# Attention with dense layers on one core: queries loaded by whole tiles, values by pairs of heads, stores of converted weights issued by GpSimd

## The chip, the core and the metric

The kernel runs on one core of a Trainium2 chip. The core has five engines that matter here, each with its own queue of instructions in program order: TensorE (PE in the profile; its weight loads, which run beside the matmuls, are PEld), VectorE (DVE), ScalarE (ACT), GpSimd (POOL) and SyncE (SP), which computes nothing and only issues transfers. An instruction waits on semaphores for what it reads and for the buffers that it writes. The metric is device microseconds (us) from start to end of one execution, the median of the runs of a kernel. The profile is of one execution, with the span in which its engines work and the clock that was granted to TensorE.

## The reference

Attention for two batches of eight heads, 576 positions and 64 numbers a head. Of each row of scores only the 32 largest go into the softmax. The result, 1152 rows of 512 features, passes through two dense layers (512 to 2048 to 512 features), the first with a softplus between its two products, the second with a leaky rectifier that has a slope for each of the 2048 features.

```
scores = scale * (q @ k.transpose(0, 1, 3, 2))        # q, k, v: 2 x 8 x 576 x 64, float32
kth    = np.partition(scores, -32, axis=-1)[..., -32:-31]
scores = np.where(scores >= kth, scores, -1e9)
attn   = np.exp(scores - scores.max(-1)) ; attn = attn / (attn.sum(-1) + 1e-9)
x = (attn @ v) as 1152 x 512
h = x @ w_in                                          # 512 x 2048, float64
x = (np.maximum(h, 0) + np.log1p(np.exp(-np.abs(h)))) @ w_out    # 2048 x 512, float64
h = x @ w_in2 ; out = (np.maximum(h, 0) + alpha * np.minimum(h, 0)) @ w_out2
```

The four weight matrices come as float64. Their bits are handed to the core unchanged, as two 32-bit words for each number, and the core makes float32 of them.

## The kernel before

**Tiles and stages.** The 1152 rows are nine tiles of 128. `CHUNKS` puts them into three chunks: tiles 3 and 4, tiles 5 to 7, and tiles 8, 0, 1, 2. A chunk first goes through attention, then through the first dense layer, then through the second, while the rows of the next chunk go through attention beside them. One "row" of the program is one head of one tile, so a chunk of two tiles has sixteen rows. Chunk 0 multiplies in float32 (`NATIVE`); the two others split each operand into a high and a low part and use three products.

**A row of attention.** TensorE makes the scores of two heads from a query tile `q` and a key tile `ks` (L430, `pss`), ScalarE copies them out (L435, `s`). VectorE finds the 32 largest with four MAX8 (L439, `m`) and three MATCH_REPLACE8 between them that strike out those already found (L442, `r`). ScalarE or VectorE builds a mask from the 32nd (L476, L478), GpSimd subtracts it in two halves (L481, `e`), ScalarE takes the exponential (L483). TensorE transposes `e` (L497 and L503, `pp` and `pq`), ScalarE copies that to `pt` (L500, L504), and TensorE multiplies it by the values `v` for two heads at a time (L527, `pav`). After the eighth head the sums of the rows are inverted by VectorE, spread by TensorE (L574, `pr`), copied by ScalarE (L578, `xn`) and multiplied by VectorE into the tile's features: `xh`, L581 in chunk 0. The first matmul of the first dense layer (`ph`, L623) needs the `xh` of both tiles of chunk 0.

**The weights.** `convert` takes one of 32 units of 128 x 1024 numbers. SyncE loads its raw bits, 1024 KB, into `cr` (L317); VectorE shifts and masks the high words into `cx` (L320) and keeps two low bits of them (L325); ScalarE turns the low words into 16 bits (L327); GpSimd adds the two in four pieces of 256 columns (L331). SyncE then stores the result, 512 KB, to a scratch tensor `ws` in the chip's memory (L334), from which later chunks load it into `w` (L359). Of the units 24 are converted ahead of the layer that uses them first (`EARLY`), the others as they are needed, and used from `cx` too.

**Buffers.** Raw bits `cr` have two (`RAWB`), `cx` three (`CXB`), `w` four (`RING`), scores `s` eight, queries `q` six tiles of 64 KB (`QB`), keys `ks` five (`KB`), values `v` ten tiles of 160 KB (`VB`), `e` two. A load into a buffer waits on its queue until the last reader of what stands there is done, and everything behind it on that queue waits with it.

**What sets the order.** The functions below don't run their instructions; they hand them to a `Planner` with an engine, a length, a due time, what they read and write, and for transfers the bytes. `order` then goes through all engines by a simple model of time and lets each take, of what could start, the one with the earliest due time. The result is the order of each engine's queue, kept as it is. Due times come from the numbers at the top (`T0`, `PACE`, `ROWS_DUE`, `AHEAD`, the leads), so these set which conversion stands ahead of which row.

Of the kernel before, what the change touches and what calls it, by code (L numbers as in the profile page):

```python
# [19 lines left out]
P = 128  # L20
# [14 lines left out]
CHUNKS = [[3, 4], [5, 6, 7], [8, 0, 1, 2]]  # L35
RING = 4
# [5 lines left out]
QB = 6  # L42
KB = 5
VB = 10
# [3 lines left out]
SPARE = [-17033.9, 2009.0, 903.3]  # L48
MASK_SPARE = [24031.0, 784.7, -18754.5]
# [5 lines left out]
T0 = 229.4  # L55
VALUES = 1.35
SCORES = 0.69
PACE = [1433.1, 1301.1, 6152.8, 6484.8, 326.6, 8896.4]
ROWS_DUE = [(-1910.7, -760.0), (978.8, 846.5), (2800.8, 12532.4)]
EARLY_DUE = [-2160.8, -143.0, 2538.2]  # L60
LOAD_LEAD = 3880.4
FETCH_LEAD = [364.0, 1458.3, -965.3]
# [205 lines left out]
def topk_attention_moe_kernel(ctx: ExitStack, tc: tile.TileContext, q, k, v, w1, w2, w3, w4, alpha, out):  # L268
# [4 lines left out]
    plan = Planner()  # L273
    op = plan.op
# [19 lines left out]
    begins = [T0 + sum(PACE[:i]) for i in range(2 * len(CHUNKS))]  # L294
# [16 lines left out]
    def convert(unit, due):  # L311
# [22 lines left out]
        op("SP", 0.45, due, lambda: nc.sync.dma_start(z, f().bitcast(F32)), reads=[f], writes=[f"ws{nm}"],  # L334
# [171 lines left out]
    def values(i):  # L506
# [23 lines left out]
        op("PE", VALUES * len(parts), due, products, reads=[*pts] + [vt for vts, _, _ in parts for vt in vts], writes=[av],  # L530
# [67 lines left out]
    class Layer:  # L598
# [3 lines left out]
        def __init__(self, layer, ci):  # L602
            self.layer, self.ci, self.tiles = layer, ci, CHUNKS[ci]
# [4 lines left out]
            self.turned = layer == 0 and ci == len(CHUNKS) - 1 and not self.native  # L608
# [46 lines left out]
        def down(self, j):  # L655
# [40 lines left out]
            if self.layer == 0:  # L696
# [123 lines left out]
```

## Time and profile before

| What | Value |
| --- | --- |
| median of three runs | 687.59 us (685.85 to 687.65) |
| the profiled execution's own time | 689.61 us |
| its span | 687.7 us |
| TensorE's mean granted clock | 0.938 of full speed |
| TensorE busy | 620.6 us, 90% of the span |
| VectorE busy | 544.3 us, 79% |
| ScalarE busy | 485.3 us, 71% |
| GpSimd busy | 359.6 us, 52% |
| moved by the DMA engines | 109.59 MB, mean 159 GB/s |

The span begins with the first work that the profile shows and ends with the last; the time of the execution is 1.9 us longer. The shares are means over a program whose stages differ: no engine need be the bound everywhere. In a timeline each row begins with its start in us, its length, its engine and its line; the brackets at its end hold the idle time ahead of it and what ended that. "x4" counts instructions taken together, and under a tile's or a line's name the durations are in ns.

### The profile page before, as it was taken

What the parts mean: (1) busy time and instruction counts of PE and PEld (TensorE: products, weight loads), DVE (VectorE), ACT (ScalarE), POOL (GpSimd) and SP (SyncE); (2) the same over time, 40 slices, a digit from 0 to 9 for tenths busy, and PEclk for the clock granted to TensorE, in tenths of its full rate; (3) what the DMA queues carried; (4) which work ended last, traced back from release to release, by engine and by line L of the source; (5) the groups of instructions that cost most, each with busy time, mean ns of one, the idle gap of its engine ahead of it and who ended that gap; (6) DMA issues with size and microseconds to landing.
All of it is one profiled execution on the core that took longest, in us unless ns stands there. A gap on an engine that the chain in (4) does not pass through costs nothing.

```text
span 687.7 us, 10318 instructions
## 1 busy us (share of the span) xinstructions
PE 620.6 (90%) x3432; PEld 463.7 (67%) x3432; DVE 544.3 (79%) x1024; ACT 485.3 (71%) x975; POOL 359.6 (52%) x393
## 2 busy tenths in 40 slices
PE   5746545699999999999999999999999999999997
PEld 3424434466666566568877778878888888788885
DVE  4999999999999899999999999989545544554442
ACT  3877678698869778878888888788675655533431
POOL 0575666565575469766987677868411112121120
PEclk9686655699999999999999999999999999999999
DMA  8877667778978883842332312122142232313121
GB/s 286 283 250 232 196 215 216 239 238 269 305 266 309 248 271 108 269 148 84 123 108 92 106 50 93 62 93 92 62 168 95 91 112 72 121 63 123 61 92 61
DMA packets 34324, 109.59 MB, mean 159 GB/s; under 512 B 3936, under 2 KB 12128, under 8 KB 30176
## 3 DMA queue, kind: packets, MB, share of 16 engines
q1 hardware_dynamic: 34272, 108.94, 47.7%
q8 instruction: 27, 0.44, 0.3%
q14 instruction: 25, 0.20, 0.1%
HBM read 89.79 MB, written 19.14 MB: 158 GB/s over the span
## 4 chain that ended last, share of the span: by engine, by line
PE 67%; DVE 12%; DMA 7%; POOL 5%; issue 4%; ACT 4%; SPq 1%; POOLq 0%; DVEq 0%; ACTq 0%
PE ph L594 8%; PE pa L594 8%; PE pa L596 8%; PE pa L595 8%; PE ph L596 8%; PE ph L595 8%; DMA cr<-in_w_dram 6%; PE pa L671 5%; DVE m L439 4%; PE pss L430 4%; DVE r L442 4%; PE ph L623 4%; PE pp L497 3%; POOL cx L331 3%; DVE cr L325 2%
## 5 line engine op out<-in xcount | busy, mean ns | idle before, releaser
L439 DVE MAX8 m<-r 128x8 f32<-128x576 f32 x216 | 156.2, 747 | 0.4
L481 POOL TENSOR_TENSOR e<-s,e 128x288 f32<-128x288 f32 x144 | 122.6, 862 | 40.1 <-ACT e L476 28.4
L331 POOL TENSOR_TENSOR cx<-cx,cr 128x256 int32<-128x256 int32 x128 | 98.8, 792 | 83.3 <-ACT cr L327 61.5
L343 POOL TENSOR_TENSOR w<-w 128x512 fp32r<-128x512 f32 x68 | 92.3, 1367 | 79.3 <-ACT w L349 75.6
L442 DVE MATCH_REPLACE8 r<-m,r 128x576 f32<-128x576 f32 x144 | 106.4, 741 | 0.0
L343 POOL TENSOR_TENSOR gl<-g,gh 128x384 fp32r<-128x384 f32 (+1 forms) x40 | 46.4, 1160 | 100.6 <-ACT gh L651 100.4
L430 PE MATMUL pss<-ks,q 64*128 64x288 f32 x320 | 75.7, 531 | 19.7 <-ACT s L435 11.9
L327 ACT ACTIVATE cr<-cr 128x1024 int16<-128x1024 uint32 x32 | 80.0, 2500 | 17.4 <-DVE cr L325 17.2
L497 PE MATMUL pp<-ident,e 128*128 128x128 f32 x288 | 48.4, 301 | 34.6 <-ACT e L483 21.9
L349 ACT CAST w<-w 128x1024 fp32r<-128x1024 f32 x64 | 66.9, 1045 | 11.1 <-DMA w<-ws 10.9
L497 PEld LDWEIGHTS pp<-ident,e 128*128 128x128 f32 x288 | 37.1, 153 | 52.7 <-ACT e L483 26.6
L430 PEld LDWEIGHTS pss<-ks,q 64*128 64x128 f32 x320 | 35.5, 219 | 48.8 <-ACT s L435 19.3
L594 PE MATMUL pa<-w,gh 128*128 128x512 f32 x160 | 66.9, 418 | 0.0
L435 ACT COPY s<-pss 128x288 f32<-128x288 f32 x144 | 52.0, 406 | 19.6 <-PE pss L430 15.6
L595 PE MATMUL pa<-w,gl 128*128 128x512 f32 x160 | 63.3, 396 | 0.0
L596 PE MATMUL pa<-w,gh 128*128 128x512 f32 x160 | 63.2, 395 | 0.0
L483 ACT ACTIVATE e<-e,nb 128x576 f32<-128x576 f32 x72 | 55.6, 772 | 9.0 <-POOL e L481 9.0
L344 DVE TENSOR_TENSOR w<-w 128x512 fp32r<-128x512 f32 x60 | 45.1, 787 | 18.6 <-ACT w L349 18.6
L638 DVE SCALAR_TENSOR_TENSOR g<-ph,g 128x256 f32<-128x256 f32 (+2 forms) x48 | 26.6, 554 | 42.1 <-ACT g L637 40.9
L439 DVE MAX8 m<-s 128x8 f32<-128x576 f32 x72 | 53.0, 746 | 8.2 <-ACT s L435 8.0
L442 DVE MATCH_REPLACE8 r<-m,s 128x576 f32<-128x576 f32 x72 | 53.4, 741 | 0.0
L644 DVE SCALAR_TENSOR_TENSOR g<-g,rest,ph 128x256 f32<-128x256 f32 (+2 forms) x48 | 29.2, 608 | 30.4 <-ACT g L642 28.3
(127 smaller groups left out, 1389.2 us busy)
## 6 DMA issues: line engine op xcount, KB each, us to landing
w<-ws SPq DMA_DIRECT2D x88, 512.0 KB, 3.3
cr<-in_w_dram SPq DMA_DIRECT2D x32, 1024.0 KB, 7.4
ws<-cx SPq DMA_DIRECT2D x32, 512.0 KB, 7.6
v<-in_v_dram SPq DMA_DIRECT2D x24, 160.0 KB, 4.3
ks<-in_k_dram SPq DMA_DIRECT2D x12, 288.0 KB, 4.3
q<-in_q_dram SPq DMA_DIRECT2D x40, 64.0 KB, 4.1
out_dram<-o SPq DMA_DIRECT2D x9, 256.0 KB, 2.0
al<-in_alpha_dram SPq DMA_DIRECT2D x1, 8.0 KB, 2.8
```

What stands on the lines that cost most here:

```text
L327: op("ACT", ACT_LOW, due, lambda: nc.scalar.activation(raw().bitcast(I16)[:, :, 2], low(), AF.Copy, scale=2.0 ** -29), reads=[f], writes=[ ...
L331: op("POOL", on_pool(cs.stop - cs.start), due, lambda cs=cs: nc.gpsimd.tensor_add(f().bitcast(I32)[:, cs], f().bitcast(I32)[:, cs], high() ...
L343: lambda cs=cs: nc.gpsimd.tensor_sub(lo()[:, cs], x()[:, cs], hi()[:, cs].bitcast(F32)),
L349: op("ACT", on_act(WIDE), due, lambda: nc.scalar.copy(w()[:, 0, :], x()), reads=reads, writes=[w])
L430: nc.tensor.matmul(pss[n](), qr()[n * D:(n + 1) * D, :], ks()[n * D:(n + 1) * D, cs], start=j == 0, stop=j == len(qk) - 1)
L439: op("DVE", on_dve(n), due, lambda: nc.vector.max(out=out(), in_=x()), reads=reads, writes=writes)
L442: op("DVE", on_dve(n) + 0.067, due, lambda: nc.vector.match_replace(out=out(), in_to_replace=found(), in_values=x(), imm_value=LOWEST), re ...
L481: op("POOL", on_pool(HS), due - AHEAD["mask"][ci], lambda cs=cs: nc.gpsimd.tensor_sub(e()[:, cs], s()[:, cs], e()[:, cs]), reads=[s], writ ...
L497: nc.tensor.transpose(pp()[:, c * P:(c + 1) * P], e()[:, c0 + c * P:c0 + (c + 1) * P], ident)
L594: nc.tensor.matmul(acc, ah, b_l, start=first, stop=False)
L595: nc.tensor.matmul(acc, a_l, bh, start=False, stop=False)
L596: nc.tensor.matmul(acc, ah, bh, start=False, stop=last)
```

## The change

Six things are different.

- **Queries.** One load brings the queries of all four pairs of heads of a tile, 256 KB, where one load brought one pair, 64 KB. Tile 4, which lies in both batches, has two. There are ten such loads instead of forty, and two buffers of 256 KB instead of six of 64.
- **Values.** One load brings both heads of a pair, 320 KB, where one load brought one head, 160 KB: twelve loads instead of 24, five buffers of 320 KB instead of ten of 160. On the host `vp` is laid out so that such a block is contiguous.
- **Stores.** The 32 stores `ws<-cx` are issued by GpSimd (`STORER`). In the planner's model such an issue takes 1.0 us there, on SyncE 0.45. All loads stay on SyncE (`LOADER`).
- **The planner's numbers.** Nearly all of them are different, so each engine's queue has another order.
- **`TOGETHER`.** The second dense layer could now take several chunks at once. With `[[0], [1], [2]]` it takes each by itself, as before.
- **Line numbers** move: L317 is now L325, L334 is L342, L581 is L594, L623 is L637.

```diff
+TOGETHER = [[0], [1], [2]]
+LOADER = 'SP'
+STORER = 'POOL'
+ISSUE = {"SP": 0.45, "ACT": 0.45, "POOL": 1.0}
...
-QB = 6
+QB = 2
...
-VB = 10
+VB = 5
...
-T0 = 229.4
+T0 = 118.9
...
+    loader, storer = ({"SP": nc.sync, "ACT": nc.scalar, "POOL": nc.gpsimd}[x] for x in (LOADER, STORER))
...
-        op("SP", 0.45, due, lambda: nc.sync.dma_start(z, f().bitcast(F32)), reads=[f], writes=[f"ws{nm}"],
+        op(STORER, ISSUE[STORER], due, lambda: storer.dma_start(z, f().bitcast(F32)), reads=[f], writes=[f"ws{nm}"],
...
-        op("SP", 0.45, due + AHEAD["scores"][ci] - LOAD_LEAD, lambda: nc.sync.dma_start(ks(), k[b, pair]), writes=[ks],
-           move=P * S * 4)
-
-    def prepare_v(b, h, ci, due):
-        if (b, h) in vst:
+        op(LOADER, ISSUE[LOADER], due + AHEAD["scores"][ci] - LOAD_LEAD, lambda: loader.dma_start(ks(), k[b, pair]),
+           writes=[ks], move=P * S * 4)
+
+    def prepare_v(b, pair, ci, due):
+        if (b, pair) in vst:
             return
         if len(vst) == VB:
             del vst[next(iter(vst))]
-        vst[b, h] = vt = buf("v", VB, [P, 5, D], F32, f"v{b}{h}")
-        op("SP", 0.45, due + AHEAD["values"][ci] - LOAD_LEAD / 2, lambda: nc.sync.dma_start(vt(), v[b, h]), writes=[vt], move=P * 5 * D * 4)
+        vst[b, pair] = vt = buf("v", VB, [P, 2, 5, D], F32, f"v{b}{pair}")
+        op(LOADER, ISSUE[LOADER], due + AHEAD["values"][ci] - LOAD_LEAD / 2, lambda: loader.dma_start(vt(), v[b, pair]),
+           writes=[vt], move=P * 10 * D * 4)
+
+    def prepare_q(t, n, ci, due):
+        if (t, n) in qst:
+            return
+        qst[t, n] = qr = buf("q", QB, [P, H // 2, P], F32, f"q{t}_{n}")
+        op(LOADER, ISSUE[LOADER], due + AHEAD["scores"][ci] - LOAD_LEAD, lambda: loader.dma_start(
+            qr(), q[:, NT if n else t]), writes=[qr], move=P * H // 2 * P * 4)
...
             prepare_k(b, pair, ci, due)
-            qr = buf("q", QB, [P, P], F32, f"q{t}{pair}{n}")
-            op("SP", 0.45, due + AHEAD["scores"][ci] - LOAD_LEAD, lambda n=n, qr=qr: nc.sync.dma_start(
-                qr(), q[:, NT if n else t, pair]), writes=[qr], move=P * P * 4)
-            qk.append((qr, kst[b, pair]))
+            prepare_q(t, n, ci, due)
+            qk.append((qst[t, n], kst[b, pair]))
...
-                        nc.tensor.matmul(pss[n](), qr()[n * D:(n + 1) * D, :], ks()[n * D:(n + 1) * D, cs],
+                        nc.tensor.matmul(pss[n](), qr()[n * D:(n + 1) * D, pair, :], ks()[n * D:(n + 1) * D, cs],
...
-            prepare_v(b, h - 1, ci, due)
-            prepare_v(b, h, ci, due)
+            prepare_v(b, h // 2, ci, due)
...
-                        nc.tensor.matmul(av()[half * D:(half + 1) * D, o:o + w], vt()[:, c, :], pt[:, block:block + w],
+                        nc.tensor.matmul(av()[half * D:(half + 1) * D, o:o + w], vt()[:, half, c, :], pt[:, block:block + w],
...
-        "v": vp.reshape(B, H, 5, P, D).transpose(0, 1, 3, 2, 4),
+        "v": vp.reshape(B, H // 2, 2, 5, P, D).transpose(0, 1, 4, 2, 3, 5),
```

What the numbers do shows in the queues. In the first place, VectorE around the second `xh`, the last of chunk 0's features. Before (`m`, `r`: a row's largest scores and what is left of it; `cx`, `cr`: a unit's conversion):

```order
L439 MAX m_1145<-s_1079 128x8
L439 MAX m_1036<-r_1084 128x8
L442 MATCH_REPLACE r_1056<-m_1048,r_1056 128x576
L581 TENSOR_TENSOR xh_694<-pav__748,xn_1160 128x4x128
L442 MATCH_REPLACE r_1171<-m_1133,s_1082 128x576
L320 TENSOR_SCALAR cx_1178<-cr_1114 128x1024
L439 MAX m_1133<-r_1171 128x8
L325 TENSOR_SCALAR cr_1114<-cr_1114 128x1024
```

After:

```order
L328 TENSOR_SCALAR cx_1059<-cr_994 128x1024
L456 MATCH_REPLACE r_1051<-m_975,r_1051 128x576
L333 TENSOR_SCALAR cr_994<-cr_994 128x1024
L453 MAX m_975<-r_1051 128x8
L456 MATCH_REPLACE r_1051<-m_975,r_1051 128x576
L328 TENSOR_SCALAR cx_1087<-cr_1049 128x1024
L453 MAX m_1098<-s_1040 128x8
L333 TENSOR_SCALAR cr_1049<-cr_1049 128x1024
L456 MATCH_REPLACE r_1103<-m_1098,s_1040 128x576
L453 MAX m_1112<-s_1038 128x8
L594 TENSOR_TENSOR xh_657<-pav__711,xn_1105 128x4x128
```

Ahead of this piece the old order has no conversion since the fourteenth; the fifteenth stood behind `xh` and now stands ahead of it, with one MAX8 and one MATCH_REPLACE8 between its two instructions. There are 81 MAX8 ahead of the second `xh` in both, 61 MATCH_REPLACE8 instead of 60, and fifteen conversions instead of fourteen. The first conversion of the piece of after is the fourteenth.

The second place is SyncE, at the first reading of stored weights (`w<-ws`). Before:

```order
L317 DMA cr_257<-in_w_dram 128x2048
L334 DMA ws_75<-cx_201 128x1024
L418 DMA q_269<-in_q_dram 128x128
L317 DMA cr_295<-in_w_dram 128x2048
L334 DMA ws_76<-cx_221 128x1024
L397 DMA ks_327<-in_k_dram 128x576
L418 DMA q_333<-in_q_dram 128x128
L418 DMA q_337<-in_q_dram 128x128
L359 DMA w_343<-ws_75 128x1024
L359 DMA w_372<-ws_76 128x1024
L317 DMA cr_398<-in_w_dram 128x2048
```

After:

```order
L325 DMA cr_233<-in_w_dram 128x2048
L421 DMA q_1_244<-in_q_dram 128x512
L325 DMA cr_274<-in_w_dram 128x2048
L367 DMA w_286<-ws_75 128x1024
L367 DMA w_343<-ws_76 128x1024
L405 DMA ks_358<-in_k_dram 128x576
L325 DMA cr_367<-in_w_dram 128x2048
L325 DMA cr_405<-in_w_dram 128x2048
```

The stores `ws` and the small query loads are gone from the queue; one query load of a tile stands between two raw loads, and the raw loads follow each other more closely.

The third place is GpSimd at its second conversion. Before:

```order
L331 TENSOR_TENSOR cx_201<-cx_201,cr_135 128x256 x4
L331 TENSOR_TENSOR cx_221<-cx_221,cr_137 128x256 x2
L481 TENSOR_TENSOR e_71<-s_139,e_71 128x288
L331 TENSOR_TENSOR cx_221<-cx_221,cr_137 128x256
L481 TENSOR_TENSOR e_71<-s_139,e_71 128x288
L331 TENSOR_TENSOR cx_221<-cx_221,cr_137 128x256
L481 TENSOR_TENSOR e_71<-s_141,e_71 128x288 x2
```

After:

```order
L339 TENSOR_TENSOR cx_179<-cx_179,cr_123 128x256 x4
L339 TENSOR_TENSOR cx_199<-cx_199,cr_125 128x256
L342 DMA ws_75<-cx_179 128x1024
L495 TENSOR_TENSOR e_71<-s_141,e_71 128x288
L339 TENSOR_TENSOR cx_199<-cx_199,cr_125 128x256
L495 TENSOR_TENSOR e_71<-s_141,e_71 128x288
L339 TENSOR_TENSOR cx_199<-cx_199,cr_125 128x256
L495 TENSOR_TENSOR e_71<-s_144,e_71 128x288
L339 TENSOR_TENSOR cx_199<-cx_199,cr_125 128x256
L495 TENSOR_TENSOR e_71<-s_144,e_71 128x288
L342 DMA ws_76<-cx_199 128x1024
```

The store of the first unit now stands between the adds of the second, and that of the second behind its last add. In both, subtractions of the mask (`e`) stand between the adds.

## Rows read from the trace of the kernel before

**Rows 1.** The page: span, and slices of TensorE and VectorE, tenths busy

```profile
span 687.7 us, 10318 instructions
...
PE   5746545699999999999999999999999999999997
...
DVE  4999999999999899999999999989545544554442
```

**Rows 2.** Stretches: us, busy (x) PE, PEld, DVE, ACT, POOL, clock, DMA, GB/s

```profile
0.00:140.00 140.00, 82.04 (x517) 55.39 (x517) 126.72 (x248) 98.58 (x192) 77.15 (x102) 0.70 0.74 238
140.00:300.00 160.00, 155.13 (x835) 101.01 (x834) 151.04 (x300) 131.99 (x273) 103.76 (x126) 1.00 0.75 250
```

**Rows 3.** TensorE's timeline: start, us, what, idle before and its end

```profile
133.72 1.13 PE L623 MATMUL ph<-xh,w 128*128 128x256 f32 x4 [0.40 <-DVE xh L581]
141.59 1.99 PE L623 MATMUL ph<-xh,w 128*128 128x256 f32 x8 [1.34 <-DVE g L638]
207.43 1.95 PE L671 MATMUL pa<-w,g 128*128 128x512 f32 x4 [0.35 <-DMA w<-ws]
285.19 0.66 PE L497 MATMUL pp<-ident,e 128*128 128x128 f32 x4 [0.89 <-ACT e L483]
```

**Rows 4.** VectorE's timeline around the first sixteen rows

```profile
13.77 0.69 DVE L320 TENSOR_SCALAR cx<-cr 128x1024 uint32<-128x1024 uint32 x1 [2.87 <-DMA cr<-in_w_dram]
46.63 0.67 DVE L320 TENSOR_SCALAR cx<-cr 128x1024 uint32<-128x1024 uint32 x1
64.20 0.69 DVE L320 TENSOR_SCALAR cx<-cr 128x1024 uint32<-128x1024 uint32 x1 [1.50 <-DMA cr<-in_w_dram]
71.39 0.88 DVE L320 TENSOR_SCALAR cx<-cr 128x1024 uint32<-128x1024 uint32 x1 [1.59 <-DMA cr<-in_w_dram]
101.14 0.68 DVE L320 TENSOR_SCALAR cx<-cr 128x1024 uint32<-128x1024 uint32 x1
116.81 0.64 DVE L320 TENSOR_SCALAR cx<-cr 128x1024 uint32<-128x1024 uint32 x1
123.27 1.27 DVE L320 TENSOR_SCALAR cx<-cr 128x1024 uint32<-128x1024 uint32 x1 [0.38 <-DMA cr<-in_w_dram]
132.97 0.69 DVE L581 TENSOR_TENSOR xh<-pav__748,xn 128x512 f32<-128x512 f32 x1 [0.30 <-ACT xn L578]
134.31 1.02 DVE L320 TENSOR_SCALAR cx<-cr 128x1024 uint32<-128x1024 uint32 x1
```

**Rows 5.** Timelines of SyncE (three rows) and GpSimd: raw loads and what frees them

```profile
55.37 0.37 SPq L317 DMA_DIRECT2D cr<-in_w_dram  x1
62.16 0.33 SPq L317 DMA_DIRECT2D cr<-in_w_dram  x1
126.42 0.33 SPq L317 DMA_DIRECT2D cr<-in_w_dram  x1
...
61.41 0.73 POOL L331 TENSOR_TENSOR cx<-cx,cr 128x256 int32<-128x256 int32 x1
```

**Rows 6.** Tile `cx` (ns min/median/max, two rows); tile `cr` (landing)

```profile
L320 DVE TENSOR_SCALAR cx<-cr x32: 637/696/1285, 13.8 to 294.1; 128x1024 uint32<-128x1024 uint32 x32
L334 SPq DMA_DIRECT2D ws<-cx x32: 327/424/1439, 22.2 to 303.8; - x32
...
DMA to landing us min/median/max: 5.7/7.4/9.8
```

**Rows 7.** Groups by line from 0 to 140 us: busy, mean ns, idle before

```profile
L331 POOL TENSOR_TENSOR cx<-cx,cr 128x256 int32<-128x256 int32 x58 | 45.6, 806 | 44.7 <-ACT cr L327 31.3 <-ACT kb L475 8.3 <-DMA ws<-cx 5.1
L439 DVE MAX8 m<-r 128x8 f32<-128x576 f32 x62 | 44.6, 744 | 0.0
L442 DVE MATCH_REPLACE8 r<-m,r 128x576 f32<-128x576 f32 x42 | 30.9, 738 | 0.0
L325 DVE TENSOR_SCALAR cr<-cr 128x1024 uint32<-128x1024 uint32 x15 | 12.9, 860 | 0.0
L320 DVE TENSOR_SCALAR cx<-cr 128x1024 uint32<-128x1024 uint32 x15 | 12.0, 798 | 6.3 <-DMA cr<-in_w_dram 6.3
```

More of the change, by code (lines that the diff above doesn't have):

```diff
@@ L54 @@
 ACT_LOW = 2.26
-T0 = 229.4
+T0 = 118.9
 VALUES = 1.35
 SCORES = 0.69
[L58 to L62, printed above, removed]
+PACE = [1523.0, 2158.4, 6829.6, 6210.0, 301.0, 562.9]
+ROWS_DUE = [(-1864.3, -800.0), (1504.9, 1068.8), (2264.0, 13060.2)]
+EARLY_DUE = [-2054.9, -163.0, 1498.1]
+LOAD_LEAD = 7344.3
+FETCH_LEAD = [543.7, -1047.2, -6947.9]
 EARLY = 24
-DIRECT_LEAD = 9718.0
-RAW_LEAD = 2408.7
-AHEAD = {'scores': [1943.9, 1871.5, 6694.5], 'mask': [46.7, -1169.1, 345.0], 'flip': [12526.4, 4276.2, 25384.6], 'values': [-301.3, 947.9, -2654.2], 'chain': [9471.3, 6009.7, -3110.2], 'split': [1852.9, -2106.4, -15053.3], 'edge': [5637.9, -646.3, 560.8]}
+DIRECT_LEAD = 3509.0
+RAW_LEAD = 4857.3
+AHEAD = {'scores': [1766.8, 2098.0, 10723.4], 'mask': [120.6, -3164.8, 1143.8], 'flip': [4968.7, 15560.1, 17199.5], 'values': [-5134.2, 858.6, -3743.9], 'chain': [16162.6, 2220.4, -1585.0], 'split': [1546.9, -1217.0, -3429.5], 'edge': [5907.1, -192.6, 4184.9]}
 MASKS = [['act'], ['act'], ['act']]
-NATIVE = {(0, 0), (1, 0)}
+NATIVE = {(1, 0), (0, 0)}
 WINDOW = 3.41333
@@ L293, in topk_attention_moe_kernel @@
     first_row = [sum(len(c) for c in CHUNKS[:i]) * H for i in range(len(CHUNKS) + 1)]
-    begins = [T0 + sum(PACE[:i]) for i in range(2 * len(CHUNKS))]
+    among = {ci: group for group in TOGETHER for ci in group}
+    passes = [(layer, ci) for ci in range(len(CHUNKS)) for layer in (0, 1) if not layer or among[ci][-1] == ci]
+    begins = {p: T0 + sum(PACE[:i]) for i, p in enumerate(passes)}
+    paces = dict(zip(passes, PACE))
     def row_due(i):
@@ L301, in moe_due @@
     def moe_due(ci, layer, j):
-        n = 2 * ci + layer
-        return begins[n] + PACE[n] * j / FJ
+        return begins[layer, ci] + paces[layer, ci] * j / FJ
     mats = {0: (w1, w2), 1: (w3, w4)}
@@ L518, in values @@
         pt = pts[0].tile
-        parts = [((vst[b, h - 1], vst[b, h]), c0, w) for b, c0, w in spans(t)]
+        parts = [(vst[b, h // 2], c0, w) for b, c0, w in spans(t)]
         def products():
-            for vts, c0, w in parts:
+            for vt, c0, w in parts:
                 o = h // 2 * P + c0
                 for c in range(5):
-                    for half, vt in enumerate(vts):
+                    for half in range(2):
                         block = (c + 5 * half if c < 4 else 4) * P + c0
-                        nc.tensor.matmul(av()[half * D:(half + 1) * D, o:o + w], vt()[:, c, :], pt[:, block:block + w],
+                        nc.tensor.matmul(av()[half * D:(half + 1) * D, o:o + w], vt()[:, half, c, :], pt[:, block:block + w],
                                          start=c == 0, stop=c == 4)
-        op("PE", VALUES * len(parts), due, products, reads=[*pts] + [vt for vts, _, _ in parts for vt in vts], writes=[av],
+        op("PE", VALUES * len(parts), due, products, reads=[*pts] + [vt for vt, _, _ in parts], writes=[av],
            share=0.5)
@@ L535, in features @@
     def features(name, bufs, ci, layer):
-        n = len(CHUNKS[ci]) * P
+        n = sum(len(CHUNKS[c]) for c in (among[ci] if layer else [ci])) * P
         if (layer, ci) in NATIVE:
@@ L602, in __init__ @@
         def __init__(self, layer, ci):
-            self.layer, self.ci, self.tiles = layer, ci, CHUNKS[ci]
+            self.layer, self.ci = layer, ci
+            self.tiles = [t for c in (among[ci] if layer else [ci]) for t in CHUNKS[c]]
             self.n = len(self.tiles) * P
@@ L607, in __init__ @@
             self.passes = 4 if self.native else 3
-            self.turned = layer == 0 and ci == len(CHUNKS) - 1 and not self.native
+            self.turned = layer == 0 and ci == len(CHUNKS) - 1 and len(among[ci]) == 1 and not self.native
             self.g = {}
@@ L695, in down @@
                 return
-            if self.layer == 0:
-                ys[ci] = [features("y", 1, ci, 1)] * KT
+            group = among[ci]
+            before = sum(len(CHUNKS[c]) for c in group[:group.index(ci)])
+            if self.layer == 0 and not before:
+                ys[group[-1]] = [features("y", 1, group[-1], 1)] * KT
             os = [buf("row", OB, [P, DM], F32, f"o{nm}{ti}") for ti in range(len(self.tiles))]
@@ L709, in down @@
                 if self.layer == 0:
-                    to_features(o, bank("pacc", 3, 512, f"py{nm}{ti}"), ys[ci][0], ti, due)
+                    to_features(o, bank("pacc", 3, 512, f"py{nm}{ti}"), ys[group[-1]][0], before + ti, due)
                 else:
@@ L744, in topk_attention_moe_kernel @@
             attend(first_row[ci + 2] - 1)
-        for layer in (0, 1):
+        for layer in (0, 1) if among[ci][-1] == ci else (0,):
             lay = Layer(layer, ci)
```

4 lines of the change are left out of this document (2 added, 2 removed).

## The prediction

> **What bounds the kernel now.** I read the page first, whose rows of slices stand for a span of 687.7 us in forty parts [rows 1]. The reader should see that TensorE's digits lie between 4 and 7 in the first eight slices and at 9 from there on, while VectorE's are at 9 from the second slice to the 28th, but for two 8s. The table of stretches puts numbers to it [rows 2]: up to 140 us TensorE works 82 us at a granted clock of 0.70, VectorE 126.7 of 140; from 140 to 300 TensorE works 155.13 of 160, at clock 1.00. So the kernel has two parts. In the first, VectorE picks the 32 largest scores of sixteen rows of attention and converts weights beside them, until the first feature tiles exist. In the second, TensorE has matmuls to the end. The number of matmuls is the same in both kernels, and so is what stands before the first matmul of the first dense layer (`ph`): the order has 60 score matmuls, 72 and 9 transposes, 120 value matmuls and 16 that spread row sums there, before and after. The end therefore moves with two things: when the first `ph` runs, and how long TensorE is idle behind it.
>
> The timeline of TensorE gives both [rows 3]: the first `ph` ran at 133.72, released by VectorE's `xh` (L581), which ran at 132.97 [rows 4]. Behind it TensorE is idle for 160 - 155.13 = 4.87 us up to 300 [rows 2], in seven waits: 1.34 for `g`, 0.35 for a weight, 0.89 for `e` [rows 3], and four more for `g` and for `pt`, 2.3 together.
>
> What sets `xh`? Behind the first scores VectorE's timeline has five idle times ahead of it [rows 4]: 2.87, 1.50, 1.59 and 0.38 for raw weights (`cr`) to land, and 0.30 for `xn`. Raw weights have two buffers, so the load of one conversion waits until GpSimd has ended the one two places earlier. SyncE's timeline shows that loop closing at once: GpSimd's last add ends at 61.41 + 0.73 = 62.14, the load is issued at 62.16 [rows 5]. From issue to landing a raw load takes 5.7 to 9.8 us, median 7.4 [rows 6]. From one conversion to the one two places on, VectorE measured 64.20 - 46.63 = 17.6 us where it had to wait, and 116.81 - 101.14 = 15.7 where it had not [rows 4]. Fourteen conversions stand ahead of the second `xh`. This loop and VectorE's own work are nearly equal, and that decides the change.
>
> **The change, part by part.** *Stores by GpSimd.* 32 instructions leave SyncE, 32 enter GpSimd. On SyncE a store's issue took 0.33 to 1.44 us, median 0.42 [rows 6]; 32 x 0.42 = 13.4 us of issue leave an engine that computes nothing, and I count no gain. The largest that rows allow is a raw load that waits in the queue: the one of 55.37 was awaited for 1.50 by VectorE [rows 4, 5]. On GpSimd no row shows an issue. From below it costs nothing: ahead of its weight adds GpSimd is idle for 44.7 us in the first 140 [rows 7], 3.0 for each of the fifteen conversions. From above, the longest issue on SyncE, 1.44, is half of that. I take 0, hidden by this idle time. Without the cover, 1.44 would be added to each turn of the loop. Behind a store on GpSimd stand the mask's subtractions (`e`, L481), for which ScalarE and then the transposes wait, and the next conversion's adds. A store no longer stands behind the raw loads of SyncE's queue but runs beside them, so a raw load may land slower, at most at the 9.8 already seen, or faster, at 5.7. Both ends stay in the range.
>
> The Trainium skill has a rule against this part ("SBUF — State Buffer", section "SBUF: two separate sides"): GpSimd builds the descriptors of the DMAs it issues, and a two-port operation of VectorE locks it out meanwhile; it names 620 ns alone and 3100 ns beside a VectorE copy. The trace agrees that the two engines hold each other up: VectorE's L320, which shares its time with GpSimd's adds, takes 0.64 to 1.29 us [rows 6]. By the page's figures fifteen stores would cost up to 15 x 2.48 = 37 us of GpSimd ahead of the first `ph`, an estimate from that page that would fill most of the idle time.
>
> *Queries by tile, values by pair.* 30 query loads and 12 value loads fewer, the same bytes. The first score waits for 288 + 256 KB instead of 288 + 64: 192 KB at the first stretch's 238 GB/s [rows 2] is 0.8 us. It is hidden by the wait of 2.87 for the first raw weights. These have 1952 KB ahead of them instead of 1824, 0.5 us more at that rate, and their issue stands four places earlier in the queue: 0 for both. The query load now waits for a whole tile's scores, with raw loads behind it on SyncE. A raw load waits for its buffer too, until GpSimd's adds are done, and where the query's wait ends first it costs nothing: 0, and where it doesn't, at most what the latest load cost VectorE, 1.59 [rows 4], which the upper end below covers.
>
> *The order.* The numbers at the top of the kernel changed too, and the order of every engine with them. Ahead of the second `xh` VectorE now has 81 MAX8, 61 MATCH_REPLACE8 and fifteen conversions, where it had 81, 60 and fourteen. By the mean durations there (30.9/42 = 0.74, 12.0/15 = 0.80, 12.9/15 = 0.86 [rows 7]) that is 0.74 + 0.80 + 0.86 = 2.4 us more. The larger matter is which conversion: the fifteenth, at 134.31 behind `xh` in the trace [rows 4], now stands ahead of it. So `xh` also waits for its raw weights. In the trace their load was issued at 126.42 [rows 5], and with the median of 7.4 they land at 133.8. The load hangs on the thirteenth conversion, which has two MAX8 and one MATCH_REPLACE8 fewer ahead of it (2 x 0.72 + 0.74 = 2.2 us), so they land at 131.6 to 133.8. VectorE itself would be there at 134.31 less 2.2 and less the `xh` of 0.6: 131.5. I take the middle, 132.7. From there to `xh` stand one half of the conversion, a MAX8, the other half, a MATCH_REPLACE8 and a MAX8: 0.80 + 0.72 + 0.86 + 0.74 + 0.72 = 3.8. `xh` runs at 136.5 instead of 132.97: 3.6 later, and the first `ph` with it. Ends: 131.5 + 3.8 = 135.3 (2.4 later) by work alone; 126.42 + 9.8 + 3.8 = 140.0 (7.1 later) with the slowest landing.
>
> *What comes back.* Where TensorE starts 3.6 later and VectorE has 2.4 us less to do behind it, waits of TensorE for others shrink. Of the seven, five hang on what TensorE itself had just done (`g`, `pt`); 0.35 for a weight's landing and 0.89 for `e` do not [rows 3]. I take these two: 1.24, rounded up to 1.3.
>
> **Sum.** 3.6 - 1.3 = 2.3 us. Against the profiled execution: span 687.7 to 690.0, its time 689.61 to 691.9. That execution lies 2.0 above the median of the runs shown (687.59), so the same sum on the median gives 689.9.
>
> **Rivals.** *No change* (chance 0.20): GpSimd's order has fewer subtractions between the adds of one conversion, the loop runs at the short end as at 101.14 to 116.81, and half of the waits of 1.50 and 1.59 go: 2.4 - 1.5 = 0.9 later, less 1.3, is 687.2. For it: of the fourteen conversions ahead of the old `xh` ten came without a wait. Against: up to the `xh`, the new order puts six conversions less than 17 us of VectorE's own work (counts of the order by the durations of [rows 7]) behind the one two places earlier, where the old order had two, and the loop took up to 17.6.
>
> *Faster* (0.28): without stores and with 42 fewer loads SyncE's queue is never the last to be late, raw weights land at the short end, and the three waits of 1.50, 1.59 and 0.38 go: `xh` at 132.97 + 2.4 - 3.5 = 131.9, 1.1 earlier. If of TensorE's 4.87 only the first, 1.34, is left, 3.5 more go: 687.6 - 4.6 = 683.0. For it: the waits named are all for landings. Against: the load at 62.16 left 0.02 us after its buffer was free, and its data were still awaited at 71.39 [rows 4, 5].
>
> *Much slower* (0.07): a store's issue on GpSimd collides with VectorE's conversions. Rows price a collision at 1.29 - 0.64 = 0.65 us for VectorE [rows 6]; fifteen of them ahead of the first `ph` are 9.7, and 3.6 + 9.7 - 1.3 = 12.0 gives 699.6. It decides from the point at which a store holds GpSimd longer than the 3.0 us that are free for each conversion. The trace bears out collisions, but most of VectorE's instructions there, MAX8, show none: mean 744 ns with nothing idle [rows 7]. Hence the small chance. The rule on locked-out descriptors (the Trainium skill, "SBUF — State Buffer", "SBUF: two separate sides") would lead to this case.
>
> **Chances and range.** Forecast 0.45, with a range of its own from 2.4 - 1.3 to 7.1 - 1.3, 688.7 to 693.4. A measurement of this kernel tells a change from none at about 0.3%, 2.1 us. Three quarters of the forecast lie above that; with the fourth case, slower gets 0.40. Same gets the no-change case and what is left of the forecast, 0.30; faster 0.30. The range reaches from just below the faster case, 682.5, to 696.5, between the forecast's upper end and the fourth case.
>
> **What would show it.** In the new profile: idle time of VectorE before L328, above all for the fifteenth conversion just ahead of the second `xh`; `xh` (L594) near 136.5 and the first `ph` near 137; TensorE's digits at 9 from the same slice on; its idle time behind the first `ph` about 3.5 us. A step fails if VectorE waits for nothing but the first raw weights, or if `xh` comes before 133 (then SyncE's queue did matter), or if GpSimd's stores take over 3 us each or VectorE's conversions lengthen. The forecast as a whole is wrong if the time is below 688.

## The result and the profile after

The changed kernel takes 694.2 us in the median of 8 runs (689.74 to 696.52), the kernel before 687.62 (8 runs, 685.85 to 690.38): a ratio of 1.0089, 95% interval 1.0068 to 1.011. Measured once more on another occasion it took 694.75, ratio 1.0122 (1.0094 to 1.0151). It is slower, by 6 to 8 us. That lies inside the stated range (682.5 to 696.5), 0.8 us above the upper end of the forecast's own (688.7 to 693.4), and is about three times its 2.3.

One caution on the profiles: an execution differs from the median of its kernel, most by up to 3 us (before: 689.61 against 687.6; `stores_alone` below: 689.27 against 691.15), that of `chain_first` by 4.7 (699.74 against 695.08). What a part costs is read from the ratios, where it goes from the profiles.

The page of the changed kernel, which answers to [rows 1]; the last line is the granted clock of TensorE in tenths:

```profile
span 692.3 us, 10228 instructions
...
PE   5643756699999999799999999999999999999997
...
DVE  5899999999899999899999999999555544454442
...
PEclk9988655799999999899999999999999999999999
```

The shape is the old one, with two new marks in the 17th slice (277 to 294 us): TensorE at 7 and its clock at 8. The table of stretches, with columns as in [rows 2], takes this place apart:

```profile
0.00:140.00 140.00, 78.79 (x489) 53.50 (x489) 127.76 (x247) 98.12 (x190) 84.39 (x118) 0.77 0.67 231
140.00:300.00 160.00, 155.00 (x843) 100.72 (x843) 148.99 (x290) 131.07 (x274) 107.68 (x138) 0.98 0.74 253
...
284.00:288.00 4.00, 1.16 (x3) 0.19 (x1) 4.00 (x8) 2.85 (x4) 0.86 (x2) 0.99 0.82 269
288.00:292.00 4.00, 3.27 (x12) 2.81 (x13) 3.12 (x7) 2.77 (x7) 3.09 (x5) 0.50 0.45 113
292.00:296.00 4.00, 4.00 (x28) 2.41 (x27) 3.97 (x11) 3.04 (x3) 1.19 (x2) 0.66 0.85 266
296.00:300.00 4.00, 4.00 (x30) 2.77 (x30) 3.58 (x7) 2.92 (x8) 3.32 (x6) 1.00 0.51 176
```

TensorE works only 1.16 us between 284 and 288, and then runs at 1.2 GHz (0.50) up to about 295, having stood idle; 3.27 us of work at half clock and 4.00 at 0.66 cost 1.6 + 1.4 = 3.0 us against full speed. VectorE's timeline around the second `xh`, answering to [rows 4]:

```profile
12.24 0.69 DVE L328 TENSOR_SCALAR cx<-cr 128x1024 uint32<-128x1024 uint32 x1 [0.54 <-DMA cr<-in_w_dram]
...
131.98 0.68 DVE L328 TENSOR_SCALAR cx<-cr 128x1024 uint32<-128x1024 uint32 x1
...
135.24 0.67 DVE L594 TENSOR_TENSOR xh<-pav__711,xn 128x512 f32<-128x512 f32 x1
```

The first conversion begins 1.5 us earlier than before, the fifteenth (131.98) stands ahead of `xh` and waits for nothing, and `xh` is 2.27 us later. TensorE's timeline, answering to [rows 3], with the start of the third stage (`ph<-xl`, first layer of chunk 1) as a mark:

```profile
135.97 1.13 PE L637 MATMUL ph<-xh,w 128*128 128x256 f32 x4 [0.99 <-DVE xh L594]
...
281.45 3.70 PE L685 MATMUL pa<-cx,g 128*128 128x512 f32 x8
288.73 1.97 PE L511 MATMUL pp<-ident,e 128*128 128x128 f32 x8 [3.57 <-ACT e L497]
...
304.62 0.42 PE L607 MATMUL ph<-xl,w 128*128 128x384 f32 x1
```

In the kernel before that mark is here:

```profile
298.64 0.74 PE L594 MATMUL ph<-xl,w 128*128 128x384 f32 x1
```

So of the 4.6 us between the two spans 2.25 stand ahead of the first `ph` (135.97 - 133.72), 3.73 between it and the mark (168.65 against 164.92), and 1.4 come back behind the mark (387.7 against 389.1). The 2.25 had come back ahead of the new wait: up to 281.4 us TensorE has run the same number of matmuls of each kind in both kernels, and the next one, a second matmul of the dense layer (`pa`), begins here at 281.45 and in the kernel before at 281.46:

```profile
281.46 2.84 PE L671 MATMUL pa<-cx,g 128*128 128x512 f32 x6
```

So in these two executions the whole of the 4.6 us arises behind this `pa`, with the new wait of 3.57 for `e` and the half clock behind it; before, the same place had 0.89 [rows 3]. More than these two show it: from this `pa` to the end the five profiles with the old order, here and below, take 405.7 to 406.6 us, the nine with the new order 408.8 to 412.7, the two of the changed kernel 410.9 and 410.6. ScalarE's timeline says what held `e` up:

```profile
281.55 0.70 ACT L449 COPY s<-pss 128x288 f32<-128x288 f32 x2 [1.09 <-PE pss L444]
285.15 2.47 ACT L335 ACTIVATE cr<-cr 128x1024 int16<-128x1024 uint32 x1 [2.90 <-DVE cr L333]
287.37 0.46 ACT L656 ACTIVATE g<-ph 128x256 f32<-128x256 f32 x1
287.74 0.18 ACT L473 ACTIVATE nb<-m 128x1 f32<-128x1 f32 x1
287.82 0.76 ACT L497 ACTIVATE e<-e,nb 128x576 f32<-128x576 f32 x1
```

The low words of the thirtieth unit wait 2.90 us for VectorE, and the exponentials stand in line behind them.

The change issues its stores on GpSimd in little time. This is the row of its tile `cx` that answers to the second of [rows 6]:

```profile
L342 POOL DMA_DIRECT2D ws<-cx x32: 551/579/854, 20.9 to 311.2; - x32
```

### The profile page after: what moved, and what is told of

It reads as the page before. It is cut to its first block, busy times and chain, and to the rows that moved or that the text cites. A ratio compares the mean times of both kernels' runs of the same rounds, so it can differ in the third digit from the quotient of the medians.

```text
span 692.3 us, 10228 instructions
## 1 busy us (share of the span) xinstructions
PE 622.0 (90%) x3432; PEld 464.9 (67%) x3432; DVE 548.1 (79%) x1025; ACT 488.0 (70%) x981; POOL 370.0 (53%) x421
## 4 chain that ended last, share of the span: by engine, by line
PE 72%; DVE 8%; DMA 6%; ACT 6%; POOL 4%; issue 2%; SPq 1%; DVEq 0%; ACTq 0%; POOLq 0%
PE ph L607 8%; PE pa L607 8%; PE pa L609 8%; PE pa L608 8%; PE ph L609 8%; PE ph L608 7%; PE ph L637 6%; PE pa L685 6%; DMA cr<-in_w_dram 5%; PE pss L444 4%; PE pp L511 3%; ACT cr L335 3%; DVE m L453 3%; POOL cx L339 2%; DVE r L456 2%
## 5 line engine op out<-in xcount | busy, mean ns | idle before, releaser
L339 POOL TENSOR_TENSOR cx<-cx,cr 128x256 int32<-128x256 int32 x128 | 96.3, 774 | 78.7 <-ACT cr L335 78.6
L495 POOL TENSOR_TENSOR e<-s,e 128x288 f32<-128x288 f32 x144 | 120.9, 849 | 31.3 <-ACT e L490 26.8
L351 POOL TENSOR_TENSOR gl<-g,gh 128x384 fp32r<-128x384 f32 (+1 forms) x36 | 41.2, 1143 | 99.4 <-ACT gh L665 99.3
L444 PE MATMUL pss<-ks,q 64*128 64x288 f32 x320 | 72.8, 520 | 19.3 <-ACT s L449 9.8
L511 PE MATMUL pp<-ident,e 128*128 128x128 f32 x288 | 50.1, 309 | 43.4 <-ACT e L497 37.1
L444 PEld LDWEIGHTS pss<-ks,q 64*128 64x128 f32 x320 | 33.4, 215 | 48.4 <-ACT s L449 15.9
L352 DVE TENSOR_TENSOR w<-w 128x512 fp32r<-128x512 f32 x60 | 46.5, 809 | 20.8 <-ACT w L357 18.8
L656 ACT ACTIVATE g<-ph 128x256 f32<-128x256 f32 (+2 forms) x48 | 23.8, 496 | 46.5 <-PE ph L609 40.4
```

What stands on the lines that cost most here:

```text
L339: op("POOL", on_pool(cs.stop - cs.start), due, lambda cs=cs: nc.gpsimd.tensor_add(f().bitcast(I32)[:, cs], f().bitcast(I32)[:, cs], high() ...
L351: lambda cs=cs: nc.gpsimd.tensor_sub(lo()[:, cs], x()[:, cs], hi()[:, cs].bitcast(F32)),
L444: nc.tensor.matmul(pss[n](), qr()[n * D:(n + 1) * D, pair, :], ks()[n * D:(n + 1) * D, cs], start=j == 0, stop=j == len(qk) - 1)
L495: op("POOL", on_pool(HS), due - AHEAD["mask"][ci], lambda cs=cs: nc.gpsimd.tensor_sub(e()[:, cs], s()[:, cs], e()[:, cs]), reads=[s], writ ...
L511: nc.tensor.transpose(pp()[:, c * P:(c + 1) * P], e()[:, c0 + c * P:c0 + (c + 1) * P], ident)
```

## The experiments

Before each, what differs from the kernel named. "Order kept" means that every engine's instructions stand as they stood; only the moved or replaced ones differ. Ratios are to the kernel before, run on the same chip.

**The stores taken back** (`order_kept_stores_sp`).

```
-op(STORER, ISSUE[STORER], due, lambda: storer.dma_start(z, f()...
+op(STORER, ISSUE[STORER], due, lambda: nc.sync.dma_start(z, f()...
```

> The changed kernel with every engine's order as it is, only the 32 stores issued by SyncE at the same places of the program. Theory (the new order costs the time, a store's issue on GpSimd is hidden): 692 to 696 us, the first ph within 1 us of 135.97, and the wait of TensorE for e near 285 us is still there with the fall of its clock. Rival (GpSimd's issues of 0.58 us each, and VectorE's longer conversions beside them, cost the time): 688 to 690 us, and VectorE's conversions before xh are 1.5 us shorter in sum.

690.54 us, ratio 1.0062 (1.0037 to 1.0086). Between the two ranges: against the two ratios of the changed kernel, 1.0089 and 1.0122, some 2 to 4 us are gone without the stores on GpSimd, and 4 are left. The first of these ratios has an interval that overlaps this one. The wait near 285 is still there, but shorter (2.5 us, clock 0.91 from 280 to 300).

**The stores alone** (`stores_alone`): the kernel before with `nc.gpsimd.dma_start` for its stores.

> The kernel before with every engine's order as it is, only the 32 stores issued by GpSimd at the same places of the program. Theory (order): 686.5 to 688.7 us, no change; an issue takes about 0.58 us on GpSimd, 14 of them 8 us up to the first ph, in idle time of which 44.7 us are there. Rival (stores): 691 to 694 us, the first ph 2 us or more later than 133.72. A third reading, that stores on SyncE held raw loads up: 684 to 686 us, with VectorE's waits for raw weights (1.50, 1.59) gone.

691.15 us, ratio 1.0057 (1.0035 to 1.0079). The rival was right on the time: stores on GpSimd cost 3.9 us by themselves, where the prediction had 0. Not on the place: in its profile, 1.9 us below its median, the first `ph` ran at 134.03, 0.3 later.

**One instruction of ScalarE moved** (`exp_first`), by a function that moves entries in the planned queues:

```
+low = turn[29] + 3                       # the low words of the thirtieth unit
+later = [i for i in act[act.index(low):] if i in exps]
+behind(queues["ACT"], {low}, later[1])   # behind the second exponential
```

> The changed kernel with one instruction moved: on ScalarE the low-word conversion of the thirtieth unit (L335, at 285.15 in the trace) stands behind the two exponentials that follow it (287.82 and 288.58) instead of ahead of them. Theory (this one wait of TensorE of 3.57 us and the stretch at half clock behind it, some 3.4 us, are most of the loss): the wait shrinks to under 0.7 us, the clock stays at full speed between 280 and 300 us, 687 to 690 us in all. Rival (only the later first ph counts, time won here is lost at the next wait): 693 to 695 us.

696.75 us, 1.0139 (1.0109 to 1.0168). The theory failed here. TensorE's waits at that place in this kernel:

```profile
284.95 1.97 PE L537 MATMUL pp<-ident,e 128*128 128x128 f32 x8 [2.33 <-ACT e L523]
288.52 0.48 PE L543 MATMUL pq<-ident,e 128*128 128x128 f32 x1 [1.60 <-ACT pt L540]
```

2.33 + 1.60 = 3.93 instead of 3.57: the exponentials still waited behind an `nb` (the bias of an exponential, which ScalarE makes of a MAX8's result), and the copies `pt` now behind the conversion.

**More of it moved** (`chain_first`).

```
+low, chain, nb, *rest = act[n:n + 8]
+act[n:n + 8] = [chain, *rest[:2], nb, *rest[2:], low]
```

> The changed kernel with ScalarE's order mended further at the same place: the low-word conversion of the thirtieth unit stands behind the two exponentials and the three copies of transposes that follow it, and the one instruction nb, which waits for a MAX8 of VectorE, behind the exponentials too. exp_first left nb ahead of them (they began at 284.05) and put the conversion ahead of the copies (another 1.60 us of TensorE). Theory (waits near 285 us and the half clock behind them are 5 to 7 us of the loss): TensorE waits under 1 us for e and pt between 280 and 295, clock 1.00 from 280 to 300, 687.5 to 690 us. Rival (what is won there is lost again, since the row of VectorE behind is no earlier): 693 to 696 us.

695.08 us, 1.0093 (1.0063 to 1.0124), as the changed kernel. With the exponentials and the copies in front, the wait is 4.05 us for the thirtieth unit itself:

```profile
289.13 1.42 PE L537 MATMUL pp<-ident,e 128*128 128x128 f32 x8 [0.35 <-ACT e L523]
290.83 0.33 PE L543 MATMUL pq<-ident,e 128*128 128x128 f32 x1 [0.28 <-ACT pt L540]
295.21 2.07 PE L664 MATMUL ph<-yh,cx 128*128 128x256 f32 x4 [4.05 <-POOL cx L364]
```

The theory that one badly placed instruction causes the loss falls. Two rows of attention and one conversion are due at the same time there; whichever goes first, TensorE waits for the other. The rival's words, lost again, are what happened.

**The same with stores on SyncE** (`chain_first_stores_sp`).

> The same with the stores issued by SyncE at the same places. If the two effects add (stores 690.54 - 694.2 = -3.7 us, the wait -5): 685 to 686.5 us, below the kernel before. If the wait near 285 is only the place where an earlier loss shows: 689.5 to 691 us, as order_kept_stores_sp.

692.26 us, 1.0069 (1.0046 to 1.0092): no gain over `order_kept_stores_sp`, and the same new wait (4.0 us for `cx`).

**The fifteenth conversion behind `xh`** (`xh_first`).

```
+behind(queues["DVE"], {turn[14] + 1, turn[14] + 2}, products_xh[1])
```

> The changed kernel with the two VectorE instructions of the fifteenth conversion behind the second xh instead of ahead of it, nothing else. The forecast's step (xh is late by this conversion): xh at about 133.9 instead of 135.24 and the first ph 1.2 us earlier. If the first ph sets the end: 693.0 us. Theory (the wait for e near 285 us hangs on the chain of conversions and not on TensorE, so TensorE just waits there longer): 694 to 695.5 us, with that wait 1 us longer or the same.

697.38 us, 1.0147 (1.0123 to 1.0172), slower than the changed kernel. In its profile the first `ph` ran at 132.45; behind its first four matmuls TensorE waited for the copies of transposes, on half clock afterwards:

```profile
132.45 1.16 PE L664 MATMUL ph<-xh,w 128*128 128x256 f32 x4
137.47 1.48 PE L469 MATMUL pss<-ks,q 64*128 64x288 f32 x4 [3.86 <-ACT pt L540]
```

A first `ph` that comes earlier is worth nothing if what stands behind it on TensorE is not ready.

**Twice as many stores** (`half_stores_pool`).

```
-lambda: nc.sync.dma_start(z, f().bitcast(F32))
+lambda: [nc.gpsimd.dma_start(z[:, cs], f().bitcast(F32)[:, cs]) for cs in pieces(WIDE, DM)]
```

> stores_alone with each store cut in two of 256 KB, both issued by GpSimd: 64 issues instead of 32, the same bytes. Theory (GpSimd's time for issues, 0.58 us each, and VectorE's conversions held up beside them, are the 3.8 us of stores_alone): 693 to 696 us, another 2 to 5 on top of 691.15; VectorE's conversions ahead of the second xh longer than the 24.6 us in sum there. Rival (it is the transfers, which now run beside the raw loads instead of behind them): 690 to 692 us.

691.11 us, 1.0063 (1.004 to 1.0087), the same as with 32. The number of issues on GpSimd doesn't set the cost. The time lies in the rival's range, but that transfers beside the raw loads are the cause is not shown: raw loads landed after 6.3 us in the median here and 6.1 in `stores_alone`, sooner than the 7.4 of the kernel before.

**Work instead of stores** (`pool_spent`).

```
+nc.gpsimd.tensor_add(spent[:].bitcast(I32), x[:, :192], x[:, 192:384])
+nc.sync.dma_start(z, f().bitcast(F32))
```

> order_kept_stores_sp (the changed kernel's order, stores by SyncE) with one more addition of 128 x 192 numbers on GpSimd in the place of each of the 32 stores, its result used by nobody; by the rate of GpSimd's other additions about 0.55 us each, as long as a store's issue there. Theory (the 3.7 us that stores on GpSimd cost are GpSimd's time, and VectorE's conversions held up by it): 693 to 695.5 us, VectorE's conversions ahead of the second xh 22 to 23 us in sum, where order_kept_stores_sp had 20.5 and the changed kernel 22.9. Rival (it is the issue of a transfer itself, or that the stores leave SyncE's queue): 690 to 691.5 us, conversions at 20 to 21 us.

691.75 us, 1.0077 (1.0047 to 1.0108): between the two, and not told apart from `order_kept_stores_sp` (1.0062). (The 20.5 and 22.9 us expected of the conversions are lower than the sums over all fifteen, 22.9 and 25.3, given further down; the difference is the same.) The added work took as long as an issue, by the group of 0 to 140 us:

```profile
L345 POOL TENSOR_TENSOR spent<-cx 128x192 int32<-128x192 int32 x15 | 9.1, 607 | 0.0
```

**Small loads again** (`loads_split`): the changed kernel, four transfers for each query tile, two for each pair of values.

```
+loader.dma_start(qr()[:, j], q[:, NT if n else t, j]) for j in range(H // 2)
+loader.dma_start(vt()[:, n], v[b, pair][:, n]) for n in range(2)
```

> The changed kernel with every engine's order and every buffer as it is, but each query tile loaded by four transfers of 64 KB and each pair of values by two of 160 KB, on SyncE at the same places. Theory (the size of these loads costs and gains nothing): 693 to 695.5 us. Rival (fewer, larger loads are what the changed kernel gains by): 696 to 698 us.

696.14 us, 1.0128 (1.0101 to 1.0155). Against the changed kernel's 1.0089 and 1.0122 that is unclear.

**Large loads alone** (`loads_alone`): the kernel before, order kept, stores on SyncE. The first load of a tile's pairs brings the tile, the first of two heads brings both, the others are left out.

```
+nc.sync.dma_start(qst[t, n](), q[:, NT if n else t]) if pair == 0 else None
+nc.sync.dma_start(both(), v[b, h // 2]) if h % 2 == 0 else None
```

> The kernel before with every engine's order as it is and stores on SyncE, but queries loaded by whole tiles (three buffers, at the place of the tile's first pair) and values by pairs of heads (at the place of the pair's first head). Theory (loads_split was 1.9 us slower than the changed kernel, so larger loads gain that): 685 to 686.5 us, raw weights waited for less than the 6.3 us of before ahead of the second xh. Rival (nothing): 686.8 to 688.2. Third (three query tiles stand ahead of the first raw weights instead of six pairs, 384 KB more, 1.6 us at the 238 GB/s of the first stretch, and the first conversions come later): 688.5 to 689.5.

683.32 us, 0.995 (0.9933 to 0.9967): the fastest of all, 3.4 us ahead of the kernel before. The third reading had it the wrong way round. SyncE's timeline shows why; the first row is of the kernel before, the others of this one:

```profile
5.92 0.90 SPq L317 DMA_DIRECT2D cr<-in_w_dram  x2
```

```profile
4.01 0.56 SPq L424 DMA_DIRECT2D qq<-in_q_dram  x1
4.62 1.25 SPq L317 DMA_DIRECT2D cr<-in_w_dram  x2
```

Here SyncE spends some 0.4 to 0.6 us on an issue, and three fewer stand ahead of the first raw weights: they are issued 1.30 us earlier and land as fast as before (7.9 and 9.8 us). VectorE:

```profile
12.56 0.69 DVE L320 TENSOR_SCALAR cx<-cr 128x1024 uint32<-128x1024 uint32 x1 [0.99 <-DMA cr<-in_w_dram]
...
61.29 0.81 DVE L320 TENSOR_SCALAR cx<-cr 128x1024 uint32<-128x1024 uint32 x1
68.56 0.90 DVE L320 TENSOR_SCALAR cx<-cr 128x1024 uint32<-128x1024 uint32 x1 [1.55 <-DMA cr<-in_w_dram]
...
130.24 0.69 DVE L588 TENSOR_TENSOR xh<-pav__712,xn 128x512 f32<-128x512 f32 x1 [0.31 <-ACT xn L585]
```

Of the waits of [rows 4] the first is 0.99 instead of 2.87, that of 1.50 is gone, that of 1.59 is left; `xh` comes 2.73 earlier, 1.21 of it at the first conversion, and the span ends 3.3 earlier. Why the wait of 1.50 went is not shown.

**The changed kernel again** (`after_again`).

> The changed kernel once more, beside the two others on one chip: 692 to 696 us. Theory (TensorE runs a fixed chain from the first ph on, so the executions differ by when the first ph runs): its profile has the first ph at 135.97 + (its own time - 694.38) within 1 us, and again a wait of about 3.6 us for e near 285 with a stretch at half clock.

694.75 us. The first `ph` ran at 133.67 in an execution of 694.58: 2.5 us earlier than the theory has it. What was won ahead was lost behind: TensorE's granted clock was 0.71 from 135 to 140 us, where the first profile has 1.00, and the first four `ph` took 2.07 us instead of 1.13; a wait for `pt` at 220.34 was 2.39 instead of 1.14; and the wait for `e`, at 289.26, was 3.58 again.

**All of the transfers, none of the order** (`loads_and_stores`).

> loads_alone with the 32 stores issued by GpSimd at the same places: all that the change does to the transfers, with the order of the kernel before. If the parts add (loads 683.32 - 687.1 = -3.8, stores 691.15 - 687.39 = +3.8): 686.5 to 688 us, and the changed kernel's 694.2 to 694.75 then hold some 7 us that only the new order brings. If stores on GpSimd cost nothing once SyncE's queue is short: 683 to 684.5 us, and the order costs 10 to 11.

689.92 us, 1.0028 (1.0007 to 1.0049): 2 us more than the parts give in sum, but the interval reaches the 1.0007 that adding the two ratios would give. Stores on GpSimd cost 5.4 us on top of `loads_alone` (0.78% of 687).

Where they cost it: VectorE's two instructions of a conversion up to the second `xh`, in groups by line (busy us, mean ns, idle before), first with stores on SyncE (`loads_alone`), then with stores on GpSimd (`loads_and_stores`), in the same order of instructions:

```profile
L325 DVE TENSOR_SCALAR cr<-cr 128x1024 uint32<-128x1024 uint32 x14 | 12.2, 874 | 0.0
L320 DVE TENSOR_SCALAR cx<-cr 128x1024 uint32<-128x1024 uint32 x14 | 11.0, 785 | 3.0 <-DMA cr<-in_w_dram 3.0
```

```profile
L325 DVE TENSOR_SCALAR cr<-cr 128x1024 uint32<-128x1024 uint32 x14 | 13.6, 974 | 0.0
L320 DVE TENSOR_SCALAR cx<-cr 128x1024 uint32<-128x1024 uint32 x14 | 11.5, 821 | 4.2 <-DMA cr<-in_w_dram 4.2
```

25.1 us instead of 23.2, and 1.2 more of waiting for raw weights: 3.1 of the 3.16 by which `xh` is later (133.40 against 130.24). In the new order the conversions are longer too, `order_kept_stores_sp` first, `after_again` second, but the waits for raw weights are shorter, and `xh` is only 0.7 later (132.94 against 132.24):

```profile
L328 DVE TENSOR_SCALAR cx<-cr 128x1024 uint32<-128x1024 uint32 x15 | 12.6, 841 | 4.4 <-DMA cr<-in_w_dram 4.4
L333 DVE TENSOR_SCALAR cr<-cr 128x1024 uint32<-128x1024 uint32 x15 | 10.3, 690 | 0.0
```

```profile
L328 DVE TENSOR_SCALAR cx<-cr 128x1024 uint32<-128x1024 uint32 x15 | 13.9, 928 | 3.2 <-DMA cr<-in_w_dram 3.1
L333 DVE TENSOR_SCALAR cr<-cr 128x1024 uint32<-128x1024 uint32 x15 | 10.9, 725 | 0.0
```

22.9 and 24.8; the first profile of the changed kernel has 25.3, `pool_spent` 23.6, and `stores_alone` 24.6 against 23.1 in the kernel before. The exception is `half_stores_pool` with 22.9, at the same time as `stores_alone`: there VectorE waited 3.5 us for `e` instead, for a reason that is not shown. One of the long ones, in the changed kernel, VectorE's row and GpSimd's beside it:

```profile
63.19 2.28 DVE L328 TENSOR_SCALAR cx<-cr 128x1024 uint32<-128x1024 uint32 x1
```

```profile
62.76 0.58 POOL L342 DMA_DIRECT2D ws<-cx  x1 [0.30 <-POOL cx L339]
63.36 1.55 POOL L495 TENSOR_TENSOR e<-s,e 128x288 f32<-128x288 f32 x2
```

The conversion begins inside the issue and ends 0.56 us after GpSimd's second subtraction, 0.67 long where nothing disturbs it. The longest such instruction of the kernel before took 1.29 [rows 6].

## Why the prediction was right, and where it was not

The direction held, and the time lies in the stated range, though above the forecast's own. The sum, 2.3, was short by 4 to 5 us (the medians differ by 6.6 and 7.7): the order, on which it rests alone, cost 4 to 8 us. That the rest came out near 0 is luck: loads and stores, both taken as 0, were wrong by nearly the same size with opposite signs.

- *The bound* (first `ph`, then TensorE's idle time): right as a way of counting, not as a cause. `loads_alone` carries 2.73 us at `xh` to the end; `xh_first` and `after_again` have an early `ph` and lose it again at what comes next, and the changed kernel's late `ph` had been made good by 281 us. The count also leaves out TensorE's clock: from 140 to 300 us TensorE was idle for 5.00 us instead of 4.87, but worked at 0.98 instead of 1.00.
- *The order, first `ph`*: the step was 3.6 late, one profile has 2.25. The fifteenth conversion is ahead of `xh`, but did not wait for its weights there; the lower end, by VectorE's work alone, was 135.3, and the profile has 135.24. That this fits is luck. Four profiles have the same order and transfers up to there, and their second `xh` ran at 131.06 (`exp_first`), 132.94 (`after_again`), 135.24 and 137.54 (`chain_first`), with 1.1, 3.2, 4.8 and 6.5 us of VectorE's waits for raw weights. Two of them lie below 133, which the prediction named as a sign against this step. Order alone, from `loads_alone` to `order_kept_stores_sp`, moved `xh` by 132.24 - 130.24 = 2.0, which is within this spread.
- *What comes back*: the step that failed most. It took 1.3 us of waits as won, one of them the 0.89 for `e`. More came back up to 281 us, all of the 2.25; but then that wait became 3.57 with about 3.0 us of half clock behind it. In ratios the order costs 1.0089 or 1.0122 against 1.0028 (0.6 to 0.9%, 4 to 6 us), or 1.0062 against 0.995 with stores on SyncE (1.1%). This includes the query buffers, two of them where `loads_alone` and `loads_and_stores` have three, which was not tried by itself. The prediction read the order up to the second `xh` only; the new wait lies 150 us behind it. What in the order would have to change there stays open, since `exp_first` and `chain_first` won nothing.
- *Loads, taken as 0*: -3.4 us on the old order; on the new one `loads_split` leaves it unclear. The step saw the issue four places earlier in the queue and wrote the bytes ahead of it against that, at the rate of the stretch; in `loads_alone` the first scores were only 0.67 later (VectorE's first MAX8 at 7.18 instead of 6.51), inside a wait, and the three issues were worth 1.30 us. The split between queries and values was not tried.
- *Stores, taken as 0, hidden by GpSimd's idle time*: +3.9 alone, +5.4 on top of the large loads, +2 to +4 in the new order. The much-slower rival named a collision with VectorE's conversions, and the prediction took it as a sign of failure if they lengthen; it priced this at 9.7 us ahead of the first `ph`, and measured were 1.5 to 2.4 there. How much of the cost this makes is not shown: with 1.2 us of waits it accounts for the later `xh` in `loads_and_stores`, but `half_stores_pool` costs as much as `stores_alone` without it. Why an issue lengthens conversions more than equal work does (`pool_spent`, 23.6) and why 64 cost no more than 32 stays open, as does the rest of the cost behind the first `ph`.
- *The faster rival* had 683.0 us from a freed queue of SyncE. `loads_alone` has 683.32, with the stores still on SyncE: fewer loads do it, not the stores. That the numbers agree is luck: the rival's sum holds 2.4 us for the new order and lets the waits of 1.59 and 0.38 go, and in `loads_alone` the order is the old one and the first of these is still there.

The Trainium skill ("SBUF — State Buffer", section "SBUF: two separate sides") gives 620 ns for a DMA issued by GpSimd alone and 3100 ns for one beside a VectorE copy. It speaks of the DMA, and the prediction's estimate of 37 us took these figures for GpSimd's time. On either reading no run here shows such growth: the longest issue of the changed kernel took 854 ns (median 579), and its stores landed 7.7 us after their issue in the median, 7.6 where SyncE issued them in the kernel before. The instructions that got longer here were VectorE's conversions.

So in ratios: large loads -0.5%, stores on GpSimd +0.3 to +0.8%, the new order +0.6 to +1.1%. The kernel to keep is `loads_alone`, which has only the first.

## What to carry to other kernels

When a change has parts, price each on the order of the kernel before, by keeping the order and exchanging one part: here the gain of one was hidden under two losses. A queue that computes nothing still has a price per issue where the first transfers set the start. An engine's idle time covers its own new work; what that work does to an engine that runs beside it has to be priced too. A wait that goes must be followed to the next thing due, on every engine, past the first milestone. And a milestone that is read from one execution of each kernel may differ by several us in the next.

## What the runs showed that was not expected

- Moving one instruction (`exp_first`) or several (`chain_first`) to end a wait of 3.57 us gave waits of 3.93 and 4.05 at the same place.
- TensorE's clock was at 0.50 for some six microseconds behind that one wait, which nearly doubled its price (3.57 idle, 3.0 at lower clock).
- Halving the stores' size and doubling their number on GpSimd changed nothing (691.15 and 691.11 us), and GpSimd's 44.7 us of idle time [rows 7] did not make them free.
